# Routed operations on VectorE and ScalarE are ordered behind the evictions written ahead of them

## The chip, the cores and the metric

The kernel runs on one core of one Trainium2 chip. The metric is the time of one execution on the device, in microseconds (us). Five engines of the core take part, each with an instruction queue of its own that it works through in order: TensorE (PE, matmuls; PEld are its weight loads), VectorE (DVE), ScalarE (ACT), GpSimd (POOL) and SyncE (SP, which issues DMAs). They meet at semaphores only. An instruction whose semaphore has not come holds up all that stands behind it in its queue.

## What is computed

A short causal convolution along the sequence (8 heads, 7 taps, weights from a softmax), and behind it a mixture of 8 experts with one expert for each token. Shortened from the reference:

```python
out = np.einsum('hk,bskhg->bshg', w, x_unf)          # x: 8 x 3584 x 192
x = out.reshape(B * S, D)                            # 28672 tokens of 192
xn = x / (np.linalg.norm(x, axis=-1, keepdims=True) + 1e-06)
en = expert_emb / (np.linalg.norm(expert_emb, axis=-1, keepdims=True) + 1e-06)
logits = xn @ en.T / tau
expert_idx = np.argmax(logits, axis=1)
gate_w = softmax(logits)[np.arange(N), expert_idx]
for e in range(8):
    h = np.maximum(x[mask] @ w1[e], 0.0)             # 192 -> 1024
    out[mask] = gate_w[mask, None] * (h @ w2[e])     # 1024 -> 192
```

## The kernel before

The tokens come in 16 chunks of 16 x 112. A chunk is **routed**: its convolution runs on PE (L431) and ACT copies the result to SBUF (L434); squares give the norms (L443 on ACT, L446 on DVE); then, four times for a quarter of the chunk each, DVE scales the tokens (L507), ACT casts them to fp16 in a wide and a narrow cast (L512, L513), and DVE writes what the casts lost (L519, L522). These rows lie in a buffer `rows2` that has two halves, one for even and one for odd chunks; DVE clears two columns of it for each chunk (L510). SP transposes a quarter by DMA (L722), PE makes logits of it (L712), and a ranking on DVE (L624 to L682) gives each token a place in its expert's list in DRAM. POOL then scatters the rows there, 16 indirect DMAs for each chunk (L728). A quarter of a chunk can write its half of `rows2` once the scatters of two chunks before have read it.

**Blocks** take rows of one expert out of that list. A block has T tokens: 128 at first, then 256, 128, 128, 256, then 384, and 512 behind the last chunk, phase by phase as chunks become ready (`PHASES`). It has two matmuls. In the first, PE fills a PSUM tile `h_ps` by five matmuls for each 128 of the 1024 hidden columns (L1002); ACT writes the relu in fp16 (L1006), DVE the residual that this fp16 lost (L1008). Each tile thus has two evictions: two such tiles at T = 128, four at T = 256, eight at T = 384 and 512. In the second, PE multiplies relu and residual by the second weights, 24 matmuls for each 128 tokens into a tile `o_ps` (L1023); ACT scales it by the gate (L1028), and POOL scatters the outputs (L1030). `h_ps` and `o_ps` share a ring of six PSUM tiles, a convolution has a ring of one. A block's relu and residual lie in one place of SBUF, which the next block's overwrite.

The program writes blocks in order, and between their steps a planner lets the generator of routed work (`dispatch`) write as many of its operations as the step's spare time on DVE and ACT pays for; `live = next(a, None)` in `run` is that call. Where the operations then stand in each engine's queue is decided by the framework's scheduler: it goes through the program with estimates of its own and puts next on each engine what it takes to be ready, older operations first. A routed operation that it takes to be ready early can so come to stand ahead of evictions that the program has written long before it. An order-only dependency (`_dep(..., False)`) adds no semaphore; it only forbids the scheduler to place an instruction ahead of another on the same engine. For PE such bounds exist (`behind`: a convolution or a logits matmul comes behind the last block matmul written ahead of it). Up to the first `PINS` = 12 blocks, all DVE and ACT operations stand behind the prologue's last one.

The names that matter: `self.last` is the last residual that a block wrote (L1008), `self.step` the last ACT eviction (L1006 or L1028).

Of the kernel before, what the change touches and what calls it, by code (L numbers as in the profile page):

```python
# [85 lines left out]
def _dep(tc, frm, to, sync=True):  # L86
    cls = mybir.DependencyClass.Sync if sync else mybir.DependencyClass.NoSync
    tc.add_manual_dep(
        frm, to, mybir.DependencyInfo(cls, mybir.DependencyReason.DATA),
        reason="routed rows are written before they are read",  # L90
    )
# [15 lines left out]
class _Moe:  # L107
# [875 lines left out]
    def block(self, T, e, xT, ids, g, gate=None):  # L983
        nc, tc = self.nc, self.tc
        nj = T // 128
        if e is None:
            wa, wb = self.slot[:, 0:W2], self.slot[:, S2:S2 + WS - W2]
            self.copy_w2()
        else:
            wa, wb = self.res[:, e * RES:e * RES + W2], self.res[:, e * RES + W2:e * RES + WS]  # L990
        w2 = wb.rearrange("p (c d) -> p c d", d=2 * D)
        hh, hl = (self.hid[:, i * NFC * T:(i + 1) * NFC * T].rearrange(
            "p (c t) -> p c t", t=T) for i in range(2))

        m = 512 // T
        for b in range(0, NFC, m):
            ps = self.ps("h", [128, m, T], F32, "h_ps")
            for c in range(m):
                for i, (o, k) in enumerate(
                        ((0, 1), (0, 0), (F, 1), (2 * F, 2), (2 * F, 3))):  # L1000
                    o += (b + c) * 128
                    mm = nc.tensor.matmul(  # L1002
                        out=ps[:, c, :], lhsT=wa[:, o:o + 128], rhs=xT[:, k, :],
                        start=(i == 0), stop=(i == 4))
            self.mm = mm.ins.name
            self.step = nc.scalar.activation(  # L1006
                out=hh[:, b:b + m, :], in_=ps, func=AF.Relu).ins
            self.last = nc.vector.scalar_tensor_tensor(  # L1008
                out=hl[:, b:b + m, :], in0=ps, scalar=0.0, in1=hh[:, b:b + m, :],
                op0=ALU.max, op1=ALU.subtract).ins.name  # L1010
            self.dt = 5 * m * T / 2400
            yield self.slack(m * T)
        if gate:
            self.copy_w1(self.at)
            gate()
        for a in range(nj):
            o = self.ps("h", [128, D], F32, "o_ps")
            q = slice(a * 128, (a + 1) * 128)
            parts = [(c, h, k) for b in range(0, NFC, m)
                     for h, k in ((hh, 0), (hh, D), (hl, 0))  # L1020
                     for c in range(b, b + m)]
            for i, (c, h, k) in enumerate(parts):
                mm = nc.tensor.matmul(  # L1023
                    out=o, lhsT=h[:, c, q], rhs=w2[:, c, k:k + D],
                    start=(i == 0), stop=(i == len(parts) - 1))
            self.mm = mm.ins.name
            y = self.op.tile([128, D], F32, tag="y", name="y")
            self.step = nc.scalar.activation(  # L1028
                out=y, in_=o, func=AF.Copy, scale=g[:, a:a + 1]).ins
            i = nc.gpsimd.indirect_dma_start(  # L1030
                out=self.out[:, :],
                out_offset=bass.IndirectOffsetOnAxis(ap=ids[a], axis=0),
                in_=y, in_offset=None, bounds_check=self.N - 1,
                oob_is_err=False).ins
            tc.declare_no_dep(i, group="out", reason="tokens are distinct")
            tc.add_to_no_dep_group("out", i)
            self.dt = 24 * D / 2400
            if gate:
                yield OUT


    def free(self, c):
        return (c in self.mixed and self.clock >= self.vacant[c % 2]
                and all((p[0] - c) % 2 for p in self.pend))
# [88 lines left out]
    def run(self):  # L1133
        self.rate = 1.0
        order = self.tc.manual_schedule(engines={self.nc.sync.engine})
        order.__enter__()
        w = self.cp.tile([H, KT], F32, name="cw")
        self.nc.sync.dma_start(out=w, in_=self.weight)
        em = self.op.tile([128, D], F32, tag="y", name="em")[0:E, :]
        self.nc.sync.dma_start(out=em, in_=self.emb)  # L1140
        tb = self.cp.tile([TP, 1], F32, name="tau_b")
        self.nc.sync.dma_start(out=tb, in_=self.tau.partition_broadcast(TP))
        self.load_x(0)
        self.constants()
        self.conv_taps(w)
        self.prep_load(0)
        self.load_x(1)
        for e in range(1, 4):
            self.prep_load(e)
        self.embeddings(em, tb)  # L1150
        warm = self.ps("h", [128, 256], F32, "warm")
        for _ in range(WARM):
            i = self.nc.tensor.matmul(out=warm, lhsT=self.idh, rhs=self.onef.bitcast(F16),
                                      start=True, stop=True)
            _dep(self.tc, i.ins, self.em_last, False)
        at = len(self.nc.cur_bb.bb.instructions)
        for v in HEAD.split():
            self.head(v)
        self.unscale()
        end = {}  # L1160
        for i in self.nc.cur_bb.bb.instructions[at:]:
            if i.engine in (self.nc.tensor.engine, self.nc.vector.engine,
                            self.nc.scalar.engine, self.nc.gpsimd.engine):
                if i.engine in end:
                    _dep(self.tc, i, end[i.engine].name, False)
                end[i.engine] = i
        self.mm = end[self.nc.tensor.engine].name
        a = self.dispatch()
        at = len(self.nc.cur_bb.bb.instructions)
        spent = [0.0, 0.0]  # L1170
        while self.ready < min(3, len(self.subs)):
            self.fetch()
        live, due, done, out = next(a, None), [0.0, 0.0], False, 0.0
        while live or self.pend or not done or self.at < len(self.subs):
            if self.at < len(self.subs):
                if self.at < PINS:
                    for i in self.nc.cur_bb.bb.instructions[at:]:
                        if i.engine in (self.nc.vector.engine, self.nc.scalar.engine):
                            _dep(self.tc, i, end[i.engine].name, False)
                    at = len(self.nc.cur_bb.bb.instructions)  # L1180
                for v in self.expert():
                    self.steer(spent)
                    self.clock += self.dt
                    out = min(1.0, out + self.pace)
                    if out >= 1.0 and self.pend:
                        self.put(self.step)
                        out -= 1.0
                    due = [min(CAP, d + self.rate * t) for d, t in zip(due, v)]
                    while live and min(due) >= 0.0:
                        held = live is WAIT  # L1190
                        if not held:
                            due = [d - t for d, t in zip(due, live)]
                            spent = [s + t for s, t in zip(spent, live)]
                        live = next(a, None)
                        if held and live is WAIT:
                            break
            else:
                self.put()
                self.clock += 1.0
                if live:  # L1200
                    live = next(a, None)
            if not live and not done:
                self.last_blocks()
                done = True
        order.__exit__(None, None, None)
        real = self.nc.values_load(self.real[0:1, 0:1], min_val=0, max_val=1 << 15)  # L1206
        with self.tc.If(real > FINAL):
            order = self.tc.manual_schedule(
                engines={self.nc.sync.engine, self.nc.vector.engine})
            order.__enter__()  # L1210
            self.subs += self.spare
            while self.at < len(self.subs):
                for _ in self.expert():
                    pass
            order.__exit__(None, None, None)
# [20 lines left out]
```

## Time and profile before

| | |
|---|---|
| runs (3): median, lowest, highest | 1286.84, 1276.65, 1290.79 us |
| profiled execution: time, span of its instructions | 1291.4, 1289.7 us |
| PE busy, weight loads busy | 1151.0 us (89%), 905.3 us (70%) |
| DVE, ACT, POOL busy | 665.5 (52%), 604.3 (47%), 530.0 us (41%) |
| mean granted clock of PE | 0.954 of full |

How to read it: the prologue (constants, weights, three chunks, eight blocks) takes the first 170 us or so. Up to about 840 us chunks are routed beside blocks; behind it only blocks are left. PE's granted clock is a share: 1.0 is 2.4 GHz, 0.5 is 1.2 GHz. "Idle before" of an instruction is the time in which its engine did nothing just ahead of it, and the arrow names what ended that; "issue" stands where the profile names nothing.

### The profile page before, as it was taken

To read this page: it belongs to the slowest core of one execution; us is meant where nothing else is said; L and a number is where in the kernel's file an instruction comes from. 1 tells how busy PE (TensorE), PEld (TensorE's weight loads), DVE (VectorE), ACT (ScalarE), POOL (GpSimd) and SP (SyncE) were. 2 spreads that over 40 slices of the span, in tenths; PEclk is the share of its full clock that TensorE was granted. 3 is DMA by queue.
4 is the path that set the end of the run, shared out by engine and by line. 5 is a ranking of instruction groups with operands and counts; after the bars stand their busy time and mean duration, and the time that the engine had idled before them with its cause. 6 is when DMAs were issued, how large, how long until landed. Compare 5 with 4: busy or idle time off the path is not lost. (4 is left out here: it accounts for less than half of the span.)

```text
span 1289.7 us, 29765 instructions
## 1 busy us (share of the span) xinstructions
PE 1151.0 (89%) x11202; PEld 905.3 (70%) x11202; DVE 665.5 (52%) x1863; ACT 604.3 (47%) x1479; POOL 530.0 (41%) x551
## 2 busy tenths in 40 slices
PE   5774998798998989899998999868999999999997
PEld 3473877586876766677776777636787878778776
DVE  5973666366545365454654737434334344445543
ACT  5973566345545545456454645213434343333333
POOL 3544245544553455355454544574222222222222
PEclk8896999899998999899999999978999999999999
DMA  9955755874966864748577574432022213221210
GB/s 250 260 115 159 144 93 137 168 160 97 183 128 149 173 124 130 169 107 185 109 159 148 121 145 103 113 87 70 29 48 51 58 39 65 65 53 33 52 45 23
DMA packets 324793, 146.64 MB, mean 114 GB/s; under 512 B 266606, under 2 KB 315117, under 8 KB 324640
## 3 DMA queue, kind: packets, MB, share of 16 engines
q1 hardware_dynamic: 300976, 93.98, 37.5%
q0 software_dynamic: 23664, 50.68, 13.6%
q8 instruction: 89, 1.46, 0.5%
q14 instruction: 64, 0.52, 0.1%
HBM read 38.35 MB, written 51.05 MB: 69 GB/s over the span
## 5 line engine op out<-in xcount | busy, mean ns | idle before, releaser
L1008 DVE SCALAR_TENSOR_TENSOR work<-h_ps,work 128x384 f16<-128x384 f32 (+1 forms) x536 | 320.0, 606 | 457.0 <-ACT work L1006 389.4
L1023 PEld LDWEIGHTS <-work 128*128 128x128 f16 x5472 | 462.6, 99 | 100.5 <-issue 47.9
L1023 PE MATMUL o_ps<-res,work 128*128 128x192 f16 x4992 | 472.0, 250 | 42.8 <-issue 23.0
L1002 PEld LDWEIGHTS <-res 128*128 128x128 f16 x3520 | 309.8, 99 | 202.0 <-issue 56.9
L1030 POOL DMA_INDIRECT out_dram<-y,id x208 | 215.4, 1036 | 455.9 <-ACT y L1028 400.2
L1006 ACT ACTIVATE work<-h_ps 128x384 f16<-128x384 f32 (+1 forms) x536 | 276.9, 533 | 245.0 <-PE h_ps L1002 176.2
L1002 PE MATMUL h_ps<-xr,res 128*128 128x384 f16 (+3 forms) x2280 | 333.7, 300 | 29.9 <-issue 22.4
L728 POOL DMA_INDIRECT rows_d<-rows,di x256 | 265.2, 1036 | 174.2 <-ACT work L1006 91.5
L1028 ACT ACTIVATE y<-o_ps,g 128x192 f32<-128x192 f32 x228 | 93.6, 418 | 253.9 <-PE o_ps L1023 152.2
L1002 PE MATMUL h_ps<-work,res 128*128 128x384 f16 (+2 forms) x1240 | 171.6, 290 | 6.8 <-issue 6.6
L431 PE MATMUL conv_ps<-xt,band 128*112 128x384 f32 x256 | 109.2, 521 | 7.0 <-issue 3.9
L434 ACT COPY xt<-conv_ps 112x384 f32<-112x384 f32 x128 | 60.5, 478 | 93.9 <-PE conv_ps L431 48.2
L443 ACT ACTIVATE sq<-xt 112x192 bf16<-112x192 f32 x196 | 70.6, 360 | 3.9
L1030 POOL DMA_INDIRECT out_dram<-y,e_mt x20 | 25.1, 1254 | 91.5 <-ACT y L1028 91.5
L512 ACT CAST rows<-xt 112x768 f16<-112x768 f32 x64 | 50.1, 828 | 20.7 <-DVE rows L510 16.9
L507 DVE TENSOR_TENSOR xt<-xt,x_p_s 112x768 f32<-112x768 f32 x64 | 58.4, 951 | 0.1
L1023 PE MATMUL o_ps<-work 128*128 128x192 f16 x480 | 46.7, 246 | 6.8 <-DVE work L850 3.3
L431 PEld LDWEIGHTS conv_ps<-xt,band 128*112 128x112 f32 x256 | 40.0, 186 | 17.9 <-issue 8.6
L1002 PE MATMUL h_ps<-xr,work 128*128 128x128 f16 x800 | 50.0, 219 | 0.3 <-issue 0.3
L513 ACT CAST rows<-xt 112x256 f16<-112x256 f32 x64 | 25.8, 405 | 48.8 <-DMA rows_d<-rows,di 34.4
L1002 PEld LDWEIGHTS <-work 128*128 128x128 f16 x800 | 46.6, 98 | 0.6 <-issue 0.4
L519 DVE TENSOR_TENSOR rows<-xt,rows 112x512 f16<-112x512 f32 x64 | 43.8, 684 | 5.1 <-ACT rows L512 5.0
(174 smaller groups left out, 601.9 us busy)
## 6 DMA issues: line engine op xcount, KB each, us to landing
xt<-in_dram SPq DMA_DIRECT2D x8, 1536.0 KB
xt<-in_dram SPq DMA_DIRECT2D x7, 1440.0 KB
res<-in_dram SPq DMA_DIRECT2D x6, 768.0 KB
rows_d<-rows,di POOLq DMA_INDIRECT x256
out_dram<-y,id POOLq DMA_INDIRECT x208
res<-in_dram SPq DMA_DIRECT2D x5, 512.0 KB
xr<-rows_d SPq DMA_TRANSPOSE x154
work<-in_dram SPq DMA_DIRECT2D x3, 512.0 KB
```

Of the source, the lines that this page charges most:

```text
L431: self.behind(nc.tensor.matmul(out=ps, lhsT=self.band[h], rhs=xt[:, :, h * G:(h + 1) * G], start=True, stop=True))
L434: nc.scalar.copy(out=xt[0:TP, :, h * G:(h + 1) * G], in_=ps)
L443: nc.scalar.activation(out=sq, in_=xc[:, t, :], func=AF.Square, accum_out=n2[:, t:t + 1])
L507: self.nc.vector.tensor_tensor(out=xc[:, u, :], in0=xc[:, u, :], in1=sb, op=ALU.mult)
L512: self.nc.scalar.copy(out=rows[:, u, 128:128 + D], in_=xc[:, u, :])
L728: i = self.nc.gpsimd.indirect_dma_start(out=self.rows_d[:, :], out_offset=bass.IndirectOffsetOnAxis(ap=idx, axis=0), in_=src, in_offset=No ...
L1002: mm = nc.tensor.matmul(out=ps[:, c, :], lhsT=wa[:, o:o + 128], rhs=xT[:, k, :], start=(i == 0), stop=(i == 4))
L1006: self.step = nc.scalar.activation(out=hh[:, b:b + m, :], in_=ps, func=AF.Relu).ins
L1008: self.last = nc.vector.scalar_tensor_tensor(out=hl[:, b:b + m, :], in0=ps, scalar=0.0, in1=hh[:, b:b + m, :], op0=ALU.max, op1=ALU.subtra ...
L1023: mm = nc.tensor.matmul(out=o, lhsT=h[:, c, q], rhs=w2[:, c, k:k + D], start=(i == 0), stop=(i == len(parts) - 1))
L1028: self.step = nc.scalar.activation(out=y, in_=o, func=AF.Copy, scale=g[:, a:a + 1]).ins
L1030: i = nc.gpsimd.indirect_dma_start(out=self.out[:, :], out_offset=bass.IndirectOffsetOnAxis(ap=ids[a], axis=0), in_=y, in_offset=None, bou ...
```

## The change

While routed work is written, the program notes what `dispatch` adds. Each new DVE instruction is put behind the last residual (`self.last`), and each new ACT instruction behind the last relu or output (`self.act`, new), that a block has written by then. Both are order-only. The whole diff:

```diff
--- before.py
+++ after.py
@@ -1005,6 +1005,7 @@
             self.mm = mm.ins.name
             self.step = nc.scalar.activation(
                 out=hh[:, b:b + m, :], in_=ps, func=AF.Relu).ins
+            self.act = self.step.name
             self.last = nc.vector.scalar_tensor_tensor(
                 out=hl[:, b:b + m, :], in0=ps, scalar=0.0, in1=hh[:, b:b + m, :],
                 op0=ALU.max, op1=ALU.subtract).ins.name
@@ -1027,6 +1028,7 @@
             y = self.op.tile([128, D], F32, tag="y", name="y")
             self.step = nc.scalar.activation(
                 out=y, in_=o, func=AF.Copy, scale=g[:, a:a + 1]).ins
+            self.act = self.step.name
             i = nc.gpsimd.indirect_dma_start(
                 out=self.out[:, :],
                 out_offset=bass.IndirectOffsetOnAxis(ap=ids[a], axis=0),
@@ -1038,6 +1040,15 @@
             if gate:
                 yield OUT
 
+
+    def routed(self, a):
+        b = self.nc.cur_bb.bb.instructions
+        at, v = len(b), next(a, None)
+        keep = {self.nc.vector.engine: self.last, self.nc.scalar.engine: self.act}
+        for i in b[at:]:
+            if i.engine in keep:
+                _dep(self.tc, i, keep[i.engine], False)
+        return v
 
     def free(self, c):
         return (c in self.mixed and self.clock >= self.vacant[c % 2]
@@ -1191,7 +1202,7 @@
                         if not held:
                             due = [d - t for d, t in zip(due, live)]
                             spent = [s + t for s, t in zip(spent, live)]
-                        live = next(a, None)
+                        live = self.routed(a)
                         if held and live is WAIT:
                             break
             else:
```

Blocks themselves get no new bound: an eviction may still be placed ahead of or behind routed operations that were written before it. SP's order is the same before and after; on POOL nine scatters stand behind one to three more outputs and two ahead of one more, out of 265.

First place, DVE at chunk 10 (T = 384): `work<-h_ps` is a residual L1008, `xt` the chunk's tokens, `rows` its rows, `pc_ps` belongs to the ranking of chunk 9. Before, all four L507 have passed earlier (in the second matmul of one block and the first of the next), and these rows stand behind the fourth of the eight residuals of a block:

```order
798 L1008 SCALAR_TENSOR_TENSOR work<-h_ps,work 128x384
799 L519 TENSOR_TENSOR rows_92<-xt,rows_92 112x4x128
800 L522 TENSOR_TENSOR rows_92<-xt,rows_92 112x4x64
801 L519 TENSOR_TENSOR rows_92<-xt,rows_92 112x4x128
802 L522 TENSOR_TENSOR rows_92<-xt,rows_92 112x4x64
803 L672 TENSOR_TENSOR off<-pc_ps,cb 112x8
804 L519 TENSOR_TENSOR rows_92<-xt,rows_92 112x4x128
805 L522 TENSOR_TENSOR rows_92<-xt,rows_92 112x4x64
806 L674 TENSOR_TENSOR cb<-pc_ps,cb 128x8
807 L677 TENSOR_TENSOR inc<-inc,off 112x128
808 L519 TENSOR_TENSOR rows_92<-xt,rows_92 112x4x128
809 L522 TENSOR_TENSOR rows_92<-xt,rows_92 112x4x64
```

And after, where the first row ends with the eighth residual of the same block:

```order
800 L1009 SCALAR_TENSOR_TENSOR work<-h_ps,work 128x384 x5
801 L507 TENSOR_TENSOR xt<-xt,x_p_s 112x768
802 L510 MEMSET rows_92 112x16x2
803 L507 TENSOR_TENSOR xt<-xt,x_p_s 112x768 x3
804 L888 SCALAR_TENSOR_TENSOR id<-e_mt,lim 128x3
805 L976 TENSOR_SCALAR g<-e_mt,res 128x3
806 L519 TENSOR_TENSOR rows_92<-xt,rows_92 112x4x128
807 L522 TENSOR_TENSOR rows_92<-xt,rows_92 112x4x64
808 L519 TENSOR_TENSOR rows_92<-xt,rows_92 112x4x128
809 L522 TENSOR_TENSOR rows_92<-xt,rows_92 112x4x64
810 L672 TENSOR_TENSOR off<-pc_ps,cb 112x8
811 L519 TENSOR_TENSOR rows_92<-xt,rows_92 112x4x128
```

The four L507 and the pairs of L519 and L522 have moved behind the block's last residual and stand together; the gate's two operations (L888, L976) are among them. Line numbers in the changed kernel are higher by one at L1009.

Second place, ACT at the same chunk: L1006 is a relu, L1028 an output, L434 the copy behind a convolution of the next chunk. Before:

```order
370 L513 CAST rows_92<-xt 112x4x64
371 L1006 ACTIVATE work<-h_ps 128x384 x4
372 L513 CAST rows_92<-xt 112x4x64
373 L1006 ACTIVATE work<-h_ps 128x384
374 L1028 ACTIVATE y<-o_ps,g 128x192 x2
375 L633 ACTIVATE ex<-l 112x128
376 L1028 ACTIVATE y<-o_ps,g 128x192
377 L1006 ACTIVATE work<-h_ps 128x384 x4
378 L513 CAST rows_92<-xt 112x4x64
379 L512 CAST rows_92<-xt 112x4x192 x4
380 L1006 ACTIVATE work<-h_ps 128x384 x4
381 L1028 ACTIVATE y<-o_ps,g 128x192 x2
```

And after, from the outputs of the block before:

```order
388 L1029 ACTIVATE y<-o_ps,g 128x192 x3
389 L633 ACTIVATE ex<-l 112x128
390 L1006 ACTIVATE work<-h_ps 128x384 x8
391 L513 CAST rows_92<-xt 112x4x64
392 L512 CAST rows_92<-xt 112x4x192 x2
393 L513 CAST rows_92<-xt 112x4x64
394 L512 CAST rows_92<-xt 112x4x192
395 L513 CAST rows_92<-xt 112x4x64
396 L512 CAST rows_92<-xt 112x4x192
397 L513 CAST rows_92<-xt 112x4x64
398 L1029 ACTIVATE y<-o_ps,g 128x192 x2
```

The narrow casts L513 have left three places between relus, and all eight casts stand behind the block's eight relus, ahead of its outputs (L1028, now L1029).

Third place, DVE at chunk 7, where blocks have T = 256 and four residuals. Before, the pairs stand behind the third one, and the four L507 have passed four blocks earlier:

```order
597 L1008 SCALAR_TENSOR_TENSOR work<-h_ps,work 128x512
598 L519 TENSOR_TENSOR rows_92<-xt,rows_92 112x4x128
599 L522 TENSOR_TENSOR rows_92<-xt,rows_92 112x4x64
600 L519 TENSOR_TENSOR rows_92<-xt,rows_92 112x4x128
601 L522 TENSOR_TENSOR rows_92<-xt,rows_92 112x4x64
602 L519 TENSOR_TENSOR rows_92<-xt,rows_92 112x4x128
603 L522 TENSOR_TENSOR rows_92<-xt,rows_92 112x4x64
604 L519 TENSOR_TENSOR rows_92<-xt,rows_92 112x4x128
605 L522 TENSOR_TENSOR rows_92<-xt,rows_92 112x4x64
606 L1008 SCALAR_TENSOR_TENSOR work<-h_ps,work 128x512
607 L888 SCALAR_TENSOR_TENSOR id<-e_mt,lim 128x2
608 L976 TENSOR_SCALAR g<-e_mt,res 128x2
```

And after, where the first row ends with the fourth:

```order
592 L1009 SCALAR_TENSOR_TENSOR work<-h_ps,work 128x512 x4
593 L888 SCALAR_TENSOR_TENSOR id<-e_mt,lim 128x2
594 L976 TENSOR_SCALAR g<-e_mt,res 128x2
595 L507 TENSOR_TENSOR xt<-xt,x_p_s 112x768
596 L510 MEMSET rows_92 112x16x2
597 L507 TENSOR_TENSOR xt<-xt,x_p_s 112x768 x3
598 L519 TENSOR_TENSOR rows_92<-xt,rows_92 112x4x128
599 L522 TENSOR_TENSOR rows_92<-xt,rows_92 112x4x64
600 L519 TENSOR_TENSOR rows_92<-xt,rows_92 112x4x128
601 L522 TENSOR_TENSOR rows_92<-xt,rows_92 112x4x64
602 L519 TENSOR_TENSOR rows_92<-xt,rows_92 112x4x128
603 L522 TENSOR_TENSOR rows_92<-xt,rows_92 112x4x64
```

Here too the L507 have joined the pairs behind the block's last residual. (One more pair follows, and then the next block's four.)

## Rows read from the trace of the kernel before

**Rows 1.** Stretches: busy us (instructions) of PE, PEld, DVE, ACT, POOL; clock, DMA share, GB/s.
```profile
214.00:560.00 346.00, 304.17 (x3088) 244.71 (x3086) 182.10 (x602) 170.27 (x454) 166.14 (x165) 0.95 0.69 146
560.00:840.00 280.00, 265.06 (x2397) 198.12 (x2395) 156.41 (x527) 144.05 (x397) 145.73 (x147) 1.00 0.63 131
```
**Rows 2.** Waits of PE, 214 to 840 us: us in total, times, longest us.
```profile
PE o_ps L1023 <- issue: 11.4, 23, 1.3
...
PE o_ps L1023 <- ACT work L1006: 8.9, 10, 2.8
...
PE o_ps L1023 <- DVE work L1008: 6.0, 11, 1.6
...
PE conv_ps L431 <- ACT xt L434: 2.9, 3, 1.0
PE h_ps L1002 <- DVE work L1008: 2.7, 3, 1.0
PE lg_ps L712 <- DMA xtb<-rows: 1.9, 2, 1.5
```

**Rows 3.** Timeline of ACT at chunk 10: start us, us, instruction, [idle before].
```profile
522.50 0.40 ACT L513 CAST rows<-xt 112x256 f16<-112x256 f32 x1 [2.66 <-DMA rows_d<-rows,di]
522.86 3.03 ACT L512 CAST rows<-xt 112x768 f16<-112x768 f32 x4
```

**Rows 4.** Timeline of DVE at chunk 10, the first and the last row of the bunch.
```profile
523.73 0.69 DVE L519 TENSOR_TENSOR rows<-xt,rows 112x512 f16<-112x512 f32 x1 [0.43 <-ACT rows L512]
...
527.83 1.01 DVE L1008 SCALAR_TENSOR_TENSOR work<-h_ps,work 128x384 f16<-128x384 f32 x2
```

**Rows 5.** Timeline of PE at chunks 9 and 10: the waits that are assigned.
```profile
475.06 0.90 PE L431 MATMUL conv_ps<-xt,band 128*112 128x384 f32 x2 [0.93 <-ACT xt L434]
...
478.26 1.67 PE L1023 MATMUL o_ps<-res,work 128*128 128x192 f16 x18 [0.83 <-DVE work L1008]
...
506.51 1.67 PE L1002 MATMUL h_ps<-xr,res 128*128 128x384 f16 x5 [1.03 <-DVE work L1008]
...
526.34 0.50 PE L1023 MATMUL o_ps<-res,work 128*128 128x192 f16 x4 [1.74 <-ACT work L1006]
528.44 2.90 PE L1023 MATMUL o_ps<-res,work 128*128 128x192 f16 x17 [1.60 <-DVE work L1008]
```

**Rows 6.** Waits of ACT, 214 to 840 us, the row of the scatters.
```profile
ACT rows L513 <- DMA rows_d<-rows,di: 34.4, 14, 4.5
```

**Rows 7.** Busy time in two stretches of low clock (columns as in rows 1).
```profile
506.60:510.00 3.40, 3.40 (x28) 2.56 (x28) 2.34 (x7) 1.50 (x5) 1.79 (x2) 0.51 0.22 65
527.10:533.90 6.80, 5.46 (x35) 5.16 (x36) 3.52 (x11) 0.32 (x1) 0.25 (x1) 0.50 1.10 199
```

**Rows 8.** Groups by line, 214 to 840 us: busy us, mean ns | idle before.
```profile
L507 DVE TENSOR_TENSOR xt<-xt,x_p_s 112x768 f32<-112x768 f32 x48 | 43.6, 949 | 0.0
L519 DVE TENSOR_TENSOR rows<-xt,rows 112x512 f16<-112x512 f32 x48 | 32.8, 684 | 5.1 <-ACT rows L512 5.0
L522 DVE TENSOR_TENSOR rows<-xt,rows 112x256 f16<-112x256 f32 x48 | 19.9, 415 | 0.0
...
L512 ACT CAST rows<-xt 112x768 f16<-112x768 f32 x48 | 36.9, 828 | 2.2 <-DVE xt L507 1.2 <-DVE rows L510 1.0
```

**Rows 9.** Timeline of DVE: first residual of a block, T = 384, 256, 128.
```profile
644.76 1.02 DVE L1008 SCALAR_TENSOR_TENSOR work<-h_ps,work 128x384 f16<-128x384 f32 x2 [7.67 <-ACT work L1006]
...
366.18 0.69 DVE L1008 SCALAR_TENSOR_TENSOR work<-h_ps,work 128x512 f16<-128x512 f32 x1 [4.53 <-ACT work L1006]
...
328.79 0.69 DVE L1008 SCALAR_TENSOR_TENSOR work<-h_ps,work 128x512 f16<-128x512 f32 x1 [3.52 <-ACT work L1006]
```

**Rows 10.** Timeline at chunk 10: SP issues transposes, PE begins the logits.
```profile
524.88 8.43 SPq L722 DMA_TRANSPOSE xtb<-rows  x4
...
549.03 0.20 PE L712 MATMUL lg_ps<-ma,xtb 128*128 128x16 f16 x2
```

**Rows 11.** Busy time where nothing is routed (columns as in rows 1).
```profile
960.00:1070.00 110.00, 110.00 (x987) 86.57 (x986) 40.58 (x86) 44.05 (x93) 25.09 (x26) 1.00 0.23 51
```

## The prediction

> **What bounds the kernel now.** I read the busy time by stretch first. Chunks are routed beside the blocks from about 214 to 840 us, the only stretch that the change can touch much: ahead of 214 us the first twelve blocks are pinned already, and behind 840 us nothing is routed. In the 346 us up to 560 PE is busy for 304.2 us, at a mean granted clock of 0.95; in the 280 us up to 840 for 265.1 us at 1.00 [rows 1]. So PE sets the pace, and the change can win only part of 42 + 15 = 57 us in which it idles, and what the clock lost. DVE and ACT are busy for about half of the stretch: they have the time, the question is when each operation gets its turn.
>
> Second, what PE waited for in that stretch [rows 2]. Four rows name an eviction or the copy behind a convolution: 8.9 + 6.0 + 2.9 + 2.7 = 20.5 us. Rows that end in "issue", o_ps alone 11.4 us, name nothing that these engines did, and I leave them where they are.
>
> Third, one place in full, the rows of chunk 10. On ACT the fourth narrow cast (L513) waits 2.66 us for scatters of an earlier chunk, out of the same row buffer, and then four wide casts (L512) run for 3.03 us [rows 3]. Four relus of a block that PE has finished stand behind them. On DVE four pairs of L519 and L522 follow, and the first residual (L1008) that stands behind those starts at 527.83 [rows 4]. PE, in its second matmul, runs dry twice: 1.74 us for an ACT eviction, 1.60 us for a DVE one [rows 5]. The waiting instruction is a cast; what is queued behind it is what PE needs.
>
> **The change part by part.** No work is added or removed: every engine has the same instructions, SP in the same order. Three things move.
>
> (a) *Row work behind the block's evictions.* In the excerpts the L512/L513 and L519/L522 of chunk 10 leave the middle of a first matmul and stand behind its eighth eviction, where DVE and ACT have the second matmul's time. Waits that held a routed operation at the front then hold nothing that PE needs, and the scatters have longer to land: L513 waits 34.4 us for them in all [rows 6]. Most of these ACT waits are hidden today, so I count gain only where PE waited. Five such waits I can assign to routed work just ahead of the eviction or copy: 0.93 and 0.83 us at chunk 9 (a cast, and an L519/L522 pair), 1.03 us at chunk 10's scale operations (two L507), and 1.74 and 1.60 us [rows 5]: 6.1 us. Of the other 20.5 - 6.1 = 14.4 us I take 40%, 5.8 us, because in small blocks an eviction that starts at once is waited for as well. Sum 11.9 us; bounds 6.1 and 20.5.
>
> (b) *The clock.* Two of those places are followed by a granted clock of half, the lower of the two levels: 3.4 us after 506.6 and 6.8 us after 527.1, with PE busy for 3.40 and 5.46 us [rows 7]. At the full level that work takes half the time: 4.4 us, if the gaps go. The low end is 0, since a later gap may do the same.
>
> (c) *What the bunch costs where it now stands.* A chunk's row work on DVE is four each of L507, L519 and L522: 4 x (0.949 + 0.684 + 0.415) = 8.2 us [rows 8]. Before, L507 and the rest stood in two places; now they stand mostly in one. The room between a block's last residual and the next block's first is 7.67 us at T = 384, 4.53 us at T = 256 and 3.52 us at T = 128 [rows 9]. So at T = 384 (seven chunks, some with rank operations in between) DVE overruns by 0.5 to 3 us. The ring of six PSUM tiles lets PE run on meanwhile, and DVE catches up, as a residual is shorter than the five matmuls that feed it. I charge 0.5 us each, 3.5 us. At chunk 7 (T = 256, third excerpt) the overrun is 8.2 - 4.5 = 3.7 us, and at chunk 6 (T = 128, seven of eight pairs and all four L507 in one place) 4.0 + 3 x 1.1 - 3.5 = 3.8 us. PE has convolutions and the next first matmul to fill with, so I charge half: 3.7 us. Sum 7.2 us; bounds 0 (all hidden) and 7 x 1.5 + 7.5 = 18 us.
>
> *What gets late.* ACT has the eight casts, 4 x (0.828 + about 0.4) = 4.9 us [rows 8], ahead of the next outputs L1028. An output holds its PSUM tile longer, and its scatter on POOL leaves later; both are covered by the ring and four y buffers. Behind the rows stand, on SP, four transposes, then the load of x and the loads of later blocks. At chunk 10 the transposes issue from 524.88 and the last is past the queue by 533.35; PE asks for the logits at 549.03 [rows 10], and in the new order at the same matmul. The last rows are done by 527.8 now; behind the block's other four residuals (2 us) and a bunch of 9 us they are done by 539, 11 us later, within the 15.7 us of room [rows 4, 10]. I charge nothing; if a chunk has no such room, it costs some 1 to 2 us, as the two waits for transposed rows that are there now (1.9 us) [rows 2].
>
> **Sum.** -11.9 - 4.4 + 7.2 = -9.1 us on the profiled execution's 1291.4 us (span 1289.7 and 1.7 around it): 1282.3 us. That execution is 4.6 us above the median of the runs, 1286.84, so for the median I forecast 1286.84 - 9.1 = 1277.7 us.
>
> **The rivals.** *1, slower: the bunch is not absorbed.* If DVE's backlog at a block's end reaches PE in full, the 18 us of (c) are paid, two half-speed spells of 3.4 us like those of [rows 7] cost 1.7 us each, and since evictions are now late for another reason only half of the 16.3 us is won: 18 + 3.4 - 8.2 = +13 us, 1300 us. It decides once the overrun outlasts what six PSUM tiles hold, thus at T = 128 and 256 first. For it: 8.2 us against rooms of 3.5 and 4.5. Against it: today DVE does an unbroken 4.4 us of L519/L522 in the middle of a block, and PE lost 3.3 us only where a DMA wait stood ahead.
>
> *2, no change: the gaps move.* PE's order changes too, and more of its waits end in "issue" than in an eviction. If the waits that go open again at a later block, (a) and (b) fall to the 6.1 us seen and (c) takes it back: -2 to +2 us, 1285 to 1289 us. For it: the two halves of the stretch idle alike for reasons not named. Against it: four of the five places named have a routed operation directly ahead.
>
> *3, much faster: lateness costs more than the gaps show.* PE could be slowed inside what counts as busy. Weight loads are busy for 198.1 of the 280 us up to 840, 71%, and for 86.6 of 110 us, 79%, where nothing is routed and PE never idles [rows 1, 11]. Were the 280 us brought to 79%, they would take 251: 29 us less, and the median 1258 us. The Trainium skill, "Perfetto Trace Analysis", "Identifying the Most-Contended Engine", says the same in general: matmul busy time is a poor measure of the distance to the ceiling, and the busy share of weight loads a better one. By that rule the 71% is headroom; by the row of PE's busy time only 15 us are. I lean on the latter, because the stretch also holds convolutions, each one load for 384 columns in fp32, which lower the share without any wait.
>
> **How the numbers follow.** Forecast (5 to 17 us less) 0.45; rival 2 (within 5) 0.25; rival 3 (over 17 less) 0.13; rival 1 (over 5 more) 0.17. One per cent, about what a measurement of this kernel can tell from none, is 12.9 us: below 1274 lies rival 3 and some two fifths of the forecast, 0.32; above 1299.7 most of rival 1, 0.12; between them 0.56. The range for 8 in 10 cuts into both outer rivals: 1261 to 1297 us; the forecast's own is 1270 to 1282.
>
> **What would show it.** Right: L513 no longer waits tens of us for scatters; the waits of PE for L1006, L1008 and L434 in 214 to 840 us fall from 20.5 to about 9 us; no half-speed spell at chunk 10's rows; the residual after a block's bunch starts 8 to 10 us after the one before. Wrong: new PE waits for L1008 of over 2 us right behind a block's end between 320 and 385 us (rival 1); the same sum of PE's idle time with other names (rival 2); weight loads above 75% in 560 to 840 us (rival 3). Waits of the logits for transposed rows above 5 us would show that rows have no room to be late.

## The result and the profile after

Over 20 runs each the changed kernel takes 1272.3 us (1265.8 to 1278.9) and the kernel before 1283.4 us (1276.7 to 1290.8): a ratio of 0.9914, with a 95% interval of 0.9898 to 0.993, 11.1 us less. The forecast was 9.1 us less, and its range holds the result. The interval leaves out a ratio of 1, and the gain lies within the bound of 1% that I counted as the same. The two profiled executions differ by more, 1289.7 to 1274.1 us of span.

In the changed kernel the residual is line L1009, the second matmul L1024, the output L1029. PE's waits in the stretch of [rows 2], with the same columns (us in total, times, longest):
```profile
PE o_ps L1024 <- issue: 10.4, 17, 2.7
PE lg_ps L712 <- DMA xtb<-rows: 10.1, 4, 4.3
...
PE o_ps L1024 <- ACT work L1006: 4.5, 6, 2.4
PE o_ps L1024 <- DVE work L1009: 4.4, 6, 2.4
PE conv_ps L431 <- ACT xt L434: 4.3, 2, 2.3
...
PE h_ps L1002 <- DVE work L1009: 1.5, 2, 1.0
```
Evictions and copies fell from 20.5 us to 4.5 + 4.4 + 4.3 + 1.5 = 14.7, a smaller fall than to the 9 or so that the prediction named as a sign. The logits now wait 10.1 us for transposed rows, where it was 1.9.

The same two stretches as in [rows 1] don't hold the same work in both kernels. So I cut both traces at the same outputs of the program (the 20th, 73rd, 117th and 135th of ACT's output operations, and some 2 us ahead of the 57th) and read the busy time between them, first of before, then of after (columns as in [rows 1]):
```profile
218.70:460.00 241.30, 208.97 (x2287) 174.93 (x2286) 130.02 (x433) 119.54 (x322) 119.77 (x117) 0.95 0.73 149
460.00:549.50 89.50, 79.99 (x662) 58.81 (x660) 45.01 (x143) 42.09 (x108) 40.38 (x42) 0.94 0.61 139
549.50:778.00 228.50, 220.01 (x1962) 162.86 (x1962) 124.81 (x410) 125.18 (x357) 117.34 (x117) 1.00 0.67 138
778.00:891.30 113.30, 92.18 (x774) 66.77 (x771) 55.31 (x155) 34.09 (x76) 65.16 (x65) 0.90 0.41 98
```
```profile
218.30:458.00 239.70, 208.34 (x2287) 176.46 (x2284) 131.72 (x440) 120.35 (x321) 116.28 (x117) 0.94 0.71 148
458.00:535.90 77.90, 75.33 (x676) 57.26 (x677) 46.82 (x140) 44.07 (x111) 41.71 (x41) 1.00 0.70 141
535.90:766.70 230.80, 221.67 (x1967) 165.83 (x1964) 127.00 (x404) 123.81 (x351) 118.97 (x118) 0.99 0.70 146
766.70:874.90 108.20, 85.46 (x780) 65.36 (x777) 56.20 (x161) 35.25 (x82) 64.09 (x65) 0.90 0.44 103
```
The first numbers to compare are the lengths: -1.6, -11.6, +2.3 and -5.1 us. The second stretch is that of chunks 9 and 10, the place worked out ahead of the result; the granted clock there rose from 0.94 to 1.00.

From the 20th to the 117th output the changed kernel is 10.9 us shorter in these two executions. PE is busy for 3.6 us less. Its waits for evictions and copies fall from 18.8 to 13.9 us, those that end in "issue" from 28.1 to 16.2, and those for transposed rows rise by 8.2. So on this chip less than half of the 11.9 us that the prediction put on evictions and copies shows under their names, and the largest fall is of waits for which the profile names no cause.

At chunk 10 the bunch now stands whole. The rows of DVE's timeline (start, us, instruction): the last residuals of a block, the first scale operation, the last operation of the rows, the next residual.
```profile
513.68 2.48 DVE L1009 SCALAR_TENSOR_TENSOR work<-h_ps,work 128x384 f16<-128x384 f32 x5
516.08 0.95 DVE L507 TENSOR_TENSOR xt<-xt,x_p_s 112x768 f32<-112x768 f32 x1
...
523.25 0.42 DVE L522 TENSOR_TENSOR rows<-xt,rows 112x256 f16<-112x256 f32 x1
...
523.86 1.02 DVE L1009 SCALAR_TENSOR_TENSOR work<-h_ps,work 128x384 f16<-128x384 f32 x2
```
The next residual starts 523.86 - 516.16 = 7.7 us after the one before ended, and PE has no wait over 0.25 us between 512 and 530 us. L513's wait for scatters, 34.4 us in [rows 6], has no row of its own any more.

### The profile page after: what moved, and what is told of

It is laid out like the page before. It is cut to its first block, busy times and chain, and to the rows that moved or that the text cites. A ratio compares the mean times of both kernels' runs of the same rounds, so it can differ in the third digit from the quotient of the medians.

```text
span 1274.1 us, 29741 instructions
## 1 busy us (share of the span) xinstructions
PE 1140.3 (89%) x11202; PEld 907.6 (71%) x11202; DVE 669.2 (53%) x1863; ACT 605.6 (48%) x1479; POOL 528.2 (41%) x551
## 4 chain that ended last, share of the span: by engine, by line
PE 45%; issue 28%; POOL 10%; ACT 5%; DMA 5%; DVE 4%; another core or an unknown queue 3%; POOLq 0%; SPq 0%; ACTq 0%; DVEq 0%
PE h_ps L1002 20%; PE o_ps L1024 18%; POOL out_dram L1032 7%; PE conv_ps L431 6%; DMA xtb<-rows 3%; POOL rows_d L728 3%; PE lg_ps L712 1%; ACT work L1006 1%; ACT sq L443 1%; DVE res L392 1%; DVE xt L507 1%; DMA rows_d<-rows,di 1%; ACT res L388 1%; ACT rows L512 1%
## 5 line engine op out<-in xcount | busy, mean ns | idle before, releaser
L1009 DVE SCALAR_TENSOR_TENSOR work<-h_ps,work 128x384 f16<-128x384 f32 (+1 forms) x536 | 319.3, 608 | 470.9 <-ACT work L1006 367.0
L1024 PEld LDWEIGHTS <-work 128*128 128x128 f16 x5472 | 463.0, 99 | 92.5 <-issue 43.1
L1024 PE MATMUL o_ps<-res,work 128*128 128x192 f16 x4992 | 466.9, 250 | 41.0 <-issue 18.5
L1006 ACT ACTIVATE work<-h_ps 128x384 f16<-128x384 f32 (+1 forms) x536 | 277.3, 533 | 279.6 <-PE h_ps L1002 201.8
L1032 POOL DMA_INDIRECT out_dram<-y,id x208 | 218.0, 1048 | 439.1 <-ACT y L1029 381.0
L1002 PE MATMUL h_ps<-xr,res 128*128 128x384 f16 (+3 forms) x2280 | 330.1, 300 | 24.0 <-issue 17.0
L728 POOL DMA_INDIRECT rows_d<-rows,di x256 | 260.3, 1017 | 166.6 <-ACT work L1006 79.7
L1029 ACT ACTIVATE y<-o_ps,g 128x192 f32<-128x192 f32 x228 | 95.0, 419 | 261.9 <-PE o_ps L1024 185.2
L1002 PE MATMUL h_ps<-work,res 128*128 128x384 f16 (+2 forms) x1240 | 168.3, 288 | 2.8 <-issue 2.8
L434 ACT COPY xt<-conv_ps 112x384 f32<-112x384 f32 x128 | 60.5, 479 | 81.5 <-PE conv_ps L431 59.0
L507 DVE TENSOR_TENSOR xt<-xt,x_p_s 112x768 f32<-112x768 f32 x64 | 58.3, 948 | 0.0
L712 PEld LDWEIGHTS <-xtb 128*128 128x128 f16 x768 | 29.6, 98 | 33.8 <-DMA xtb<-rows 16.8
L1024 PE MATMUL o_ps<-work 128*128 128x192 f16 x480 | 46.5, 246 | 7.7 <-DVE work L850 3.3
L519 DVE TENSOR_TENSOR rows<-xt,rows 112x512 f16<-112x512 f32 x64 | 43.8, 685 | 7.9 <-ACT y L1029 4.8
```

Source lines behind the costliest of these rows:

```text
L434: nc.scalar.copy(out=xt[0:TP, :, h * G:(h + 1) * G], in_=ps)
L507: self.nc.vector.tensor_tensor(out=xc[:, u, :], in0=xc[:, u, :], in1=sb, op=ALU.mult)
L728: i = self.nc.gpsimd.indirect_dma_start(out=self.rows_d[:, :], out_offset=bass.IndirectOffsetOnAxis(ap=idx, axis=0), in_=src, in_offset=No ...
L1002: mm = nc.tensor.matmul(out=ps[:, c, :], lhsT=wa[:, o:o + 128], rhs=xT[:, k, :], start=(i == 0), stop=(i == 4))
L1006: self.step = nc.scalar.activation(out=hh[:, b:b + m, :], in_=ps, func=AF.Relu).ins
L1009: self.last = nc.vector.scalar_tensor_tensor(out=hl[:, b:b + m, :], in0=ps, scalar=0.0, in1=hh[:, b:b + m, :], op0=ALU.max, op1=ALU.subtra ...
```

## The experiments

The theory: row work ahead of evictions is what cost, and most at chunks 9 and 10, since in the order before their L519/L522 follow the 124th and 148th residual, four short of a first matmul's end, while at chunks 11 to 13 they stand at a block's end already (176, 200, 232). The rivals: the gain is spread over all routed operations; or any reshuffle would do.

The twelve runs went to three other chips, all faster than the first: the kernel before takes 1207.7 us on the one of rows_only, rest_only, act_only and only_9_10, 1204.5 us on that of after_again, but_9_10, gap3 and turn12, and 1207.0 us on that of mid, turn12_to5, turn12_5 and before_again. Each ratio is to the kernel before on the same chip.

### Which operations

A list `made[c]` collects what `scaled` and `rest` issue for chunk c; the lines that fill it are left out of the diffs.

**rows_only**, the row work alone is bound:
```diff
-            if i.engine in keep:
+            if i.engine in keep and any(i is v for r in self.made.values() for v in r):
```


> Only the row work of a chunk (L507, L510, L512, L513, L519, L522) is ordered behind the block's last eviction; squares, ranking and convolution copies are free as before. Theory A (row work ahead of the evictions is what cost): the whole gain, 1270 to 1275 us beside 1283 of before. Theory B (the gain is spread over all routed operations): about half, 1277 to 1279. Theory C (any reshuffle of the order would have moved the time, nothing in particular did): no particular value, so within 1283 +/- 6.

**rest_only**, with `not any(...)` in the same place:

> The counterpart: everything but the row work is ordered behind the evictions, the row work is free as before. Theory A: no change, 1281 to 1286 us. Theory B: about half the gain, 1277 to 1279. Theory C: within 1283 +/- 6.

Measured: rows_only 0.9889 (0.9869 to 0.991), 1193.5 us; rest_only 1.0012 (0.9995 to 1.0028), 1208.0 us. The row work is all of it. The order of squares, ranking and copies moves nothing, and it reshuffles the queues as well, so "any reshuffle" falls too.

**act_only**, the bound on ScalarE alone:
```diff
-        keep = {self.nc.vector.engine: self.last, self.nc.scalar.engine: self.act}
+        keep = {self.nc.scalar.engine: self.act}
```


> The order is kept for ScalarE alone. The casts then stand where the change puts them, L519 and L522 with them since they read the casts, and the scale operations (L507) stay ahead, some 12 to 16 evictions earlier, as before. If late casts and what reads them carry the gain: 1271 to 1275 us, less than 2 us from the change. If the L507 ahead of the evictions matter as much (PE waited 1.03 us for them at chunk 10, and a spell at half the clock followed): 1275 to 1279.

Measured: 0.9912 (0.9893 to 0.9931), 1197.1 us. Casts held by their own queue hold L519 and L522 as well, which read them; the L507 of chunks 7 to 13 stay 2 to 16 evictions ahead. This is most of the gain. What the L507 still cost shows in PE's waits:
```profile
PE o_ps L1024 <- DVE work L1009: 4.7, 4, 1.4
PE h_ps L1002 <- DVE work L1009: 2.8, 4, 1.3
```
These 7.5 us are 1.2 in the changed kernel (below). The difference in time to rows_only, 0.0023, is inside the intervals.

### Which chunks

**only_9_10**:
```diff
-            if i.engine in keep:
+            if i.engine in keep and any(i is v for c in (9, 10) for v in self.made[c]):
```


> Only the row work of chunks 9 and 10 is ordered behind the evictions. In the order before, these two alone stand four evictions ahead of the end of a first matmul; the others stand at a block's end or one to three evictions ahead of it. In the two profiles the stretch between the outputs around these two chunks (460 to 549 us of before) holds 11.6 us of the 15.6 that the profiled runs differ by. Theory A, sharpened to two places: 1272 to 1276 us. Theory B or a gain spread over all chunks: two chunks of twelve, 1280 to 1282.

**but_9_10**, with `not any(...)`, and **after_again**, the changed kernel as it is:

> The change without the row work of chunks 9 and 10, which stay free (L519 and L522 three evictions ahead of a block's end for chunk 9, two for chunk 10). Only these two chunks gave 0.9934 (0.9913 to 0.9956). Theory A at two places: the rest is worth under 0.3%, 0.997 to 1.000. Theory B, gain spread over chunks 4 to 10: what only_9_10 left, 0.994 to 0.996.

> The changed kernel itself, as the anchor for the kernels beside it. On the chip of the first four runs the kernel before took 1207.7 us instead of 1283 (PE waits that end in issue are nearly gone there), and ordering the row work alone gave a ratio of 0.9889 (0.9869 to 0.991). If the order of squares, ranking and copies adds nothing, this gives the same: 0.987 to 0.992.

Measured: only_9_10 0.9934 (0.9913 to 0.9956), but_9_10 0.9944 (0.9914 to 0.9973), after_again 0.9897 (0.9871 to 0.9924). So the place theory was half right: by the times, two chunks of twelve carry about half, some 8 us, and the others some 7, where theory A left them under 4 us. The two parts add up to the whole within their intervals. The one trace of each doesn't bear out the half: PE's waits for evictions and copies between the outputs that the next section uses are 18.5 us in only_9_10, whose profiled execution (1209.5 us) is the slowest of its eleven, and 5.0 in but_9_10, beside 20.8 before. By the waits the other chunks carry most of it; how much lies where is not settled.

### Where the time goes

**before_again**, the kernel before:

> The kernel before itself, one look for its trace on the chip of these runs. Its PE waits for evictions between the outputs of block 14 and the end of the routing should be 18 to 22 us, its waits for transposed rows 12 to 16, and none that end in issue over 1 us, as in the profile of the kernel that orders all but the row work.

It ran in 1207.5 us, and its waits came out as expected. I set it beside after_again, on another chip of nearly the same speed, between the same outputs (the 20th and the 129th): 200.2 to 780.3 us here, 200.6 to 769.0 us there. It is one execution of each. PE's waits (us in total, times, longest), before_again first:
```profile
PE lg_ps L712 <- DMA xtb<-rows: 13.7, 5, 7.5
PE o_ps L1023 <- DVE work L1008: 9.4, 11, 3.1
PE o_ps L1023 <- ACT work L1006: 7.5, 3, 4.6
PE h_ps L1002 <- DVE work L1008: 2.3, 4, 0.7
PE conv_ps L431 <- ACT xt L434: 1.6, 2, 0.9
PE o_ps L1023 <- issue: 0.2, 1, 0.2
```
```profile
PE lg_ps L712 <- DMA xtb<-rows: 19.3, 10, 5.5
PE h_ps L1002 <- DMA work<-rows_d: 2.0, 2, 1.1
PE h_ps L1002 <- DVE work L1009: 1.0, 1, 1.0
PE conv_ps L431 <- ACT xt L434: 0.7, 1, 0.7
PE o_ps L1024 <- DVE work L1009: 0.2, 1, 0.2
PE lg_ps L712 <- issue: 0.2, 1, 0.2
```
The busy time of the same two stretches (columns as in [rows 1]):
```profile
200.20:780.30 580.10, 545.25 (x5428) 435.83 (x5427) 336.75 (x1105) 317.13 (x840) 311.01 (x310) 0.97 0.72 149
```
```profile
200.60:769.00 568.40, 545.05 (x5446) 438.11 (x5445) 343.38 (x1106) 320.28 (x840) 305.46 (x310) 0.97 0.74 153
```
PE is busy for the same 545 us at the same mean clock, 0.97. The 11.7 us are idle time alone: evictions and copies 20.8 to 1.9, that is -18.9; transposed rows +5.6; rows of the blocks +2.0. Waits that end in "issue" are 0.2 us in each. Sum -11.3, beside -11.7 of length. Of these 11.7 us, 4.8 lie in the stretch of chunks 9 and 10 (101.3 us to 96.5).

Chunk 7 shows what such a wait was, in before_again, on the timeline of ACT and then on that of PE:
```profile
325.02 0.40 ACT L513 CAST rows<-xt 112x256 f16<-112x256 f32 x1 [6.73 <-DMA rows_d<-rows,di]
325.33 0.59 ACT L1006 ACTIVATE work<-h_ps 128x512 f16<-128x512 f32 x1
```
```profile
325.98 1.46 PE L1023 MATMUL o_ps<-res,work 128*128 128x192 f16 x8 [4.61 <-ACT work L1006]
```
A cast waits 6.73 us for scatters; the relu behind it takes 0.6 us; PE, which needs what the relu writes, loses 4.61 us. On ACT nothing but this cast lies between that relu and the one before. In all, L513 waits 50.7 us for scatters in the stretch of before_again and 42.7 in that of rest_only, where the row work is free; in rows_only, act_only, after_again and mid its wait for them has no row.

### A wait or a bunch

**mid**: routed work is handed out only behind first-matmul steps.
```diff
-                    while live and min(due) >= 0.0:
+                    while live and min(due) >= 0.0 and v is not OUT:
```


> The change, with routed work handed out behind first-matmul steps alone, never behind an output of the second matmul. A chunk's quarters then follow the evictions of a first matmul one by one, inside the block (chunk 9 behind evictions 131 to 134, chunk 10 behind 154 to 157), and about as late as in the change, so that the scatters have landed. If what cost before was the wait for the scatters ahead of evictions (theory W): few waits for evictions, under 8 us, and 0.988 to 0.994. If it was row work in the middle of a first matmul as such (theory M): 13 to 20 us of waits for evictions as before, 0.997 to 1.003.

Measured: 1.0031 (1.0008 to 1.0054), 1209.6 us, with these waits of PE over the same outputs:
```profile
PE lg_ps L712 <- DMA xtb<-rows: 25.7, 16, 6.9
PE h_ps L1002 <- DMA xr<-rows_d: 6.7, 2, 4.6
PE o_ps L1024 <- ACT work L1006: 0.9, 1, 0.9
PE o_ps L1024 <- DVE work L1009: 0.6, 1, 0.6
```
On the waits, theory W holds: 1.5 us for evictions with the row work inside first matmuls. On the time both theories were wrong about what decides: the work comes later, and transposed rows (25.7) and the blocks' rows (6.7) take back all that was won. As the quarters of chunks 9 and 10 are spread here, one per eviction, this doesn't say what a bunch of 8 us inside a first matmul would cost without a wait; that was not tried.

### What the late rows cost

Chunk 5 in after_again, on the timeline of SP and then on that of PE:
```profile
254.32 0.36 SPq L930 DMA_DIRECT2D e_mt<-rows_d  x1
254.86 12.57 SPq L722 DMA_TRANSPOSE xtb<-rows  x4
```
```profile
260.26 0.22 PE L712 MATMUL lg_ps<-ma,xtb 128*128 128x16 f16 x2 [5.45 <-DMA xtb<-rows]
...
264.69 0.22 PE L712 MATMUL lg_ps<-ma,xtb 128*128 128x16 f16 x2 [3.95 <-DMA xtb<-rows]
```
The first quarter's L522 ended at 248.0 us and the last at 251.8, but SP was issuing the row loads of seven blocks, some 4 us each, until 254.7; then the four transposes took 12.6 us to issue. The Trainium skill, "DMA: Bandwidth & Descriptors", "Silent corruption: two transposing streams in flight at once", says that transposes of different queues must not be in flight together; no run here shows it, and by it a second queue would be no remedy. What I tried instead is to ask later. In program order the logits come TURN = 7 us of PE time behind the last transpose, and their four groups GAP = 0.5 us apart.

**gap3**, the groups 3 us apart:
```diff
             yield 0.2, 0.2
-            yield self.clock + GAP
+            yield self.clock + 3.0
```


> The change, with the four logits groups of a chunk offered 3.0 us of PE time apart instead of 0.5. With the row work ordered, PE waited 19.1 us in 11 places for transposed rows at its logits (L712) on the chip of the first runs; the transposes leave SP 2 to 4 us apart, so at least the waits of the second to fourth group, 9 us of the 19.1, go if they are real time of PE: ratio 0.981 to 0.986. If PE is delayed elsewhere instead, because ranking and scatters come later and the planner moves the row work by a block: 0.988 to 0.994.

**turn12**, and **turn12_to5** and **turn12_5**, which take `c < 6` and `c == 5`:
```diff
-            yield self.clock + TURN
+            yield self.clock + (12.0 if c < 9 else TURN)
```


> The change, with the first logits group of chunks 3 to 8 offered 12 us of PE time behind the last transpose instead of 7. It takes away the waits at the first group, 10 us of the 19.1 (6.8 at chunk 5 alone, where the transposes stand on SP behind the row loads of seven blocks). If they are real time of PE: 0.980 to 0.985. If the later ranking gives it back: 0.988 to 0.994.

> As turn12, but for chunks 3 to 5 alone; chunks 6 to 8 keep 7 us. turn12 had the PE 20 us ahead at the 48th output of its profiled run and lost 10 of them where blocks waited for their rows (9.8 us in two waits), since the later chunks were ranked later. If only the later chunks' delay fed those waits: 0.980 to 0.986. If blocks starve whenever PE is earlier, because the supply of rows sets the pace there: 0.987 to 0.992.

> As turn12, for chunk 5 alone, whose first logits group waited 5.5 to 8.4 us for transposed rows in every profile of the ordered kernels. If that wait is real time of PE: 4 to 6 us less than the change, 0.985 to 0.987. If it is given back: 0.988 to 0.992.

Measured: gap3 1.0059 (1.0036 to 1.0083), turn12 0.9895 (0.9864 to 0.9927), turn12_to5 0.9819 (0.9795 to 0.9843), 1185.0 us, turn12_5 0.9975 (0.9952 to 0.9998). The rows of PE's waits for DMAs, of gap3, of turn12_to5 and of turn12_5:
```profile
PE h_ps L1002 <- DMA xr<-rows_d: 19.5, 3, 11.3
PE h_ps L1002 <- DMA work<-rows_d: 6.5, 1, 6.5
...
PE lg_ps L712 <- DMA xtb<-rows: 1.1, 2, 0.8
```
```profile
PE lg_ps L712 <- DMA xtb<-rows: 7.8, 2, 5.4
PE h_ps L1002 <- DMA xr<-rows_d: 4.2, 1, 4.2
PE h_ps L1002 <- DMA work<-rows_d: 3.6, 1, 3.6
```
```profile
PE lg_ps L712 <- DMA xtb<-rows: 24.2, 8, 9.1
PE conv_ps L431 <- DMA xt<-in_dram: 5.5, 1, 5.5
```
gap3 does what it should, 19.3 to 1.1 us at the logits, and pays 26.0 us where blocks wait for rows that were ranked too late. turn12 for chunks 3 to 8 comes out even with the change; for chunks 3 to 5 alone it beats both kernels: 0.9819 beside 0.9897, 1185.0 us. That the later chunks' delay fed the blocks' waits is borne out as to the time, less so by the waits, which stay (7.8 us beside 9.8). turn12_5 is a miss: the wait for chunk 5's rows stayed (5.8 us), one of 9.1 us came up at chunk 6, whose transposes now start on SP 10.2 us behind the first quarter's L522, with row loads of blocks between them, where it was 4.6 us in after_again; and one of 5.5 us for x. So here a delay at one chunk moved what stands behind it on SP. Why c = 5 alone does harm and 3 to 5 together help is not settled. Of the 13.2 us of span by which turn12_to5 is shorter than after_again, 5.9 lie ahead of the 20th output, thus ahead of chunk 5: that output comes at 194.7 us there, at 200.6 in after_again and at 201.5 in turn12_5.

## Why the prediction was right, and where not

Right in sign and mechanism. That the size is right as well is luck: it is the sum of four terms that were each off. The forecast is for the first chip; measured is the ledger between before_again and after_again, on two others, where almost no wait ends in "issue":

| term | forecast, us | measured, us |
|---|---|---|
| (a) waits for evictions and copies | -11.9 (-6.1 to -20.5) | -18.9 |
| (b) the clock | -4.4 (0) | 0 |
| (c) the bunch | +7.2 (0 to 18) | 1.9 at most, counted in (a)'s remainder |
| transposed rows and rows of the blocks | 0 (1 to 2 at a chunk without room) | +7.6 |
| sum | -9.1 | -11.3 |

*(a)* The cause stands: rows_only and rest_only show it, and chunk 7 shows the waiting cast. The five waits that I assigned and the clock behind them, 6.1 + 4.4 = 10.5 us at chunks 9 and 10, came to 11.6 us in the profiled executions of the first chip. By the ledger, the step that failed is the 40% that I took of the waits without a name, "because in small blocks an eviction that starts at once is waited for as well". Hardly any are: 1.9 of 20.8 us are left in the ledger. That fits the some 7 us that chunks other than 9 and 10 won. On the first chip 14.7 us are left, so there the 40% was not too little. But 7.2 of them are the three longest waits, and in each it is ACT that sat idle, for 2.6 to 4.1 us, with no row work ahead of what PE waited for; one of them, on the timeline of ACT and then on that of PE:
```profile
562.87 0.87 ACT L1006 ACTIVATE work<-h_ps 128x384 f16<-128x384 f32 x2 [4.07 <-PE h_ps L1002]
```
```profile
564.01 0.41 PE L1024 MATMUL o_ps<-res,work 128*128 128x192 f16 x3 [2.43 <-DVE work L1009]
```
By this profile the matmuls that the two relus read had ended by 561.6 us. What held ACT then it doesn't name.

*(b)* On the first chip the half-speed spells at chunk 10 went, as said: 0.94 to 1.00 at 79.99 and 75.33 us of busy time, 4.7 us less, near the 4.4. But other spells came, one of 3 us behind a wait of 2.3 us at 746.6 us. Read in windows of 1 us between the 20th and the 117th output, PE was busy at the lower level for some 27 us before and 28 after, and the mean clock of the whole run went from 0.954 to 0.951. In the ledger the mean clock is 0.97 in both kernels, and the gain is as large. So the low end, 0, was the better value: a later gap did do the same.

*(c)* The step that failed is the overrun charged to PE. At chunk 10 the gap between residuals, 7.7 us, is near what the sum of the row work said (8.2) and just under the 8 to 10 named as a sign, and PE lost nothing: tiles of the ring and a convolution fed it. At chunks 6 and 7, where I charged 3.7 us, after_again has one wait of 0.7 us for a copy, and the first chip one of 2.0, for a copy behind the casts. (At chunk 6 three of the four pairs stand in one place, as the sum of the prediction has it; its words "seven of eight" are a slip.) No wait for L1009 came between 320 and 385 us on the first chip, and rival 1 fell with it.

*What gets late.* Charged with nothing, since chunk 10 had 15.7 us of room. That one chunk stood for all was the mistake: at chunks 3 to 5, in blocks of 128 and 256 tokens, the transposes queue behind row loads on SP and the logits already waited (13.7 us in before_again). The sign of it that I named, over 5 us of such waits, came: 10.1 us on the first chip, 19.3 in after_again. With the blocks' rows it took back 7.6 of the 18.9 us that (a) gave.

Of the rivals, 2 (gaps move under other names) is partly true: 7.6 us of waits for DMAs came where 18.9 us went. Rival 3 is not: weight loads in 560 to 840 us were busy for 198.12 us before and 197.49 after, 71% both. In the ledger's stretches they fill 435.83 of 580.1 us, 75%, and 438.11 of 568.4, 77%; in turn12_to5, at 1185.0 us, the same work has them at 438.47 of 559.4 us, 78%. By the rule of the Trainium skill, "Perfetto Trace Analysis", "Identifying the Most-Contended Engine", that the busy share of weight loads tells better than that of matmuls how far the ceiling is, headroom was left at 77%. The faster turn12_to5 agrees with it.

## What to carry to other kernels

In an engine's queue a waiting instruction costs what stands behind it: look for work that needs a DMA, and ask what PE needs next on that queue; an order without a wait of its own can give 1%. Work that is held back arrives later, so read the room of its next consumer at the worst chunk, not at the best, and on the queue that issues the DMA. Where terms of both signs add up, name each one's sign in the trace: a right sum proves none of them.

## What was not expected of the hardware

The same program takes 6% longer on the first chip than on the three others. Of the 83.9 us by which the span of before is longer than that of before_again, PE is idle for 46.9 and busy for 37.0. PE's waits that end in "issue" make 65.5 us of the one span and 0.2 of the other, and they come also ahead of anything the change touches. PE's waits between the first and the 13th output on the first chip, and one weight-load group of its page (busy, mean ns | idle before), and then that group in before_again:
```profile
PE h_ps L1002 <- issue: 16.2, 17, 1.9
```
```profile
L1002 PEld LDWEIGHTS <-res 128*128 128x128 f16 x3520 | 309.8, 99 | 202.0 <-issue 56.9
```
```profile
L1002 PEld LDWEIGHTS <-res 128*128 128x128 f16 x3520 | 308.2, 99 | 163.2 <-issue 16.3
```
Between those two outputs 90.6 us passed on the first chip and 75.6 us in before_again. What these waits are the profile doesn't name. The ratio of the change is nearly the same with and without them, 0.9914 and 0.9897.
